# Halving 44 matmuls of the first MLP product in each chunk

## The chip, the cores and the metric

The kernel runs on one core of one Trainium2 chip. The metric is the device time of one execution in microseconds (us); a kernel's time is the median of its runs. One more execution was taken by the hardware profiler, and everything said below about single instructions comes from that one. Engines are named as the profile names them: PE is TensorE's matmul, PEld its weight load, DVE is VectorE, ACT is ScalarE, POOL is GpSimd and SP is SyncE.

## The reference

The program is an RWKV-7 recurrence followed by a two-layer MLP with exact gelu, all in fp32. For each of 4 batches and 8 heads a 40x40 state is carried over 768 steps; the rows of the result, 3072 tokens of 320 values, go through the MLP.

```python
for t in range(S):
    ...
    y[:, :, t] = np.einsum('bhd,bhde->bhe', rt, state)
    Sa = np.einsum('bhde,bhe->bhd', state, at)
    state_decay = state * wt[:, :, None, :] - np.einsum('bhd,bhe->bhde', Sa, bt)
    state = state_decay + np.einsum('bhd,bhe->bhde', vt, kt)
...
h = x @ w_in                                   # 3072x320 by 320x2048
g = 0.5 * h * (1.0 + erf(h * inv_sqrt2))
return (g @ w_out).astype(np.float32)          # 3072x2048 by 2048x320
```

## The kernel before

The 768 steps are cut into 12 chunks (NCH) of 64 (C). Within a chunk the recurrence is written as matrix products for all heads and batches; only the state goes from chunk to chunk. The main loop (line 1244) runs over chunks 2 to 11; chunks 0 and 1 are written out before it, mixed with the conversion of the weights.

**The recurrence's products.** Most go through the helper `mm` (line 110) and are small, 32 or 64 rows by 32 or 64 columns, so that four of them fit on the 128x128 array side by side, each on its own tile of the array. They are named after their PSUM tile: `J` and `J2` (lines 784 to 800), `X` (816), `sap` (828), `saT_ps` (839), `QY` (862 and 874), `M_ps`, `A_ps`, `RV_ps` and `N_ps` (584), `wT_ps` and `cum` (435 and 439), `av` (644). Four products in a row on four different tiles are the rule; `saT_ps` is the exception, since its loop goes over rows e^x in the order 0, 1, 1, 0, so that two products in a row fall on one tile. `tn_ps` (lines 459 and 915) are 8 transposes of 128x128.

**The MLP.** `mlp(c)` (line 985) is a generator. For each quarter q of the 2048 hidden values it makes one PSUM tile `ph` with 20 matmuls (line 993): two blocks s of hidden values, five blocks kt of 64 inputs, two halves x. Half x uses the rows x\*64 to x\*64+63 of the array, of `w_in_sb` and of `xt`, and writes to its own PSUM bank `ph[:, x]`; so two matmuls can run at once, on the upper and the lower half of the array. The moving operand has TB = 256 columns (two groups g of 128 tokens). ACT then takes gelu of the tile into `gt` (line 995). Chunks 0 to 2 finish with a plain second product (line 1010); from chunk 3 (NS) on, `seven` (line 936) makes it with seven block products in place of eight (line 946), 112 matmuls of 160 columns.

**The order of the work.** All queues follow the order of the program text; nothing is moved by a scheduler. `pieces` holds generators of `mlp`, and `fill()` (line 1024) runs the oldest up to its next `yield`, so that a piece of MLP stands between two steps of the recurrence. In a chunk of the main loop PE's order is J, X, a piece of ph, J2, a piece of ph, sap, saT_ps, a piece of ph, the first part of QY, M_ps, a piece of ph, the rest of QY, and then pieces of the second product (`po`) between A_ps, wT_ps, cum, tn_ps, av, RV_ps and N_ps.

**In the machine's program** an fp32 matmul is two passes, each a weight load (LDWEIGHTS) and a matmul (MATMUL) of its own, one after the other. The four instructions of one matmul stand together.

Of the kernel before, what the change touches and what calls it, by code (L numbers as in the profile page):

```python
# [19 lines left out]
def kernel(  # L20
# [46 lines left out]
    nc = tc.nc  # L67
    B, H, S, D = r.shape
    DM, DF = moe_w_in.shape
    P = 128  # L70
# [5 lines left out]
    G = B // 2  # L76
    NCH = S // C
    NF = DF // P
    TB = G * P
    NK = -(-DM // HP)  # L80
# [15 lines left out]
    def duo(name):  # L96
        pt = psum.tile([P, 2, 512], FP32, tag="duo", name=name)
        while asked:
            n = asked.pop()
            mm(pt[:, 0, :n * P], ident, cum_m.unsqueeze(1).to_broadcast([P, n, P]))  # L100
        return pt

    def half(j, n=HP):
        return slice(j * HP, j * HP + n)
# [37 lines left out]
    NS = 3  # L142
# [155 lines left out]
    w_in_sb = const.tile([P, NK, DF // 2], FP32, name="w_in_sb")  # L298
# [620 lines left out]
    def block(g, z):  # L919
        return gt[:, z * NF // 2:(z + 1) * NF // 2, g * P:(g + 1) * P]  # L920
# [12 lines left out]
    def half_tile(tag, bufs):  # L933
        return work.tile([P, NF // 2, P], FP32, tag=tag, name="half", bufs=bufs)
# [47 lines left out]

    gts = {}

    def mlp(c):
        xt = xts.pop(c)
        for q in range(NF // 4):
            ph = duo("ph").rearrange("p x (s t) -> p x s t", s=2)
            for s in range(2):
                p = 2 * q + s  # L990
                for kt in range(NK):
                    for x in range(2):
                        nc.tensor.matmul(ph[:, x, s], w_in_sb[half(x), kt, p * P:(p + 1) * P], xt[half(x), kt],  # L993
                                         start=kt == 0, stop=kt == NK - 1)
            nc.scalar.activation(gt[:, 4 * q:4 * q + 4].rearrange("p (x s) t -> p x s t", x=2), ph, ACT.Gelu)  # L995
            if c >= NS and q == NF // 4 - 1:
                s1, s2 = half_tile("conv", 2), None
                nc.vector.tensor_tensor(s1, block(1, 0), block(1, 1), ALU.add)  # L998
                if c >= NCH - 2:
                    s2 = half_tile("conv", 2)  # L1000
                    nc.vector.tensor_tensor(s2, s1, block(0, 0), ALU.subtract)
            yield
        if c >= NS:
            yield from seven(c, s1, s2)
            return
        po = duo("po")[:, :, :DM]
        for part in range(2):
            for g in range(G):
                for f in range(NF // 2 * part, NF // 2 * (part + 1)):
                    nc.tensor.matmul(po[:, g], gt[:, f, g * P:(g + 1) * P], w_out_sb[:, f],  # L1010
                                     start=f == 0, stop=f == NF - 1)
                for last in range(G if part and g else 0):
                    os = work.tile([P, DM], FP32, tag="os", name="os", bufs=2)
                    nc.vector.tensor_copy(os, po[:, last])
                    for e in range(2):
                        row = (G * e + last) * S + c * C
                        nc.sync.dma_start(out=out[row:row + C], in_=os[half(e)])
                yield
# [118 lines left out]
    fetch(2, "k", k, nc.sync)  # L1137
    fetch_inverse(1)
    pieces.append(mlp(0))
    turn_v(1)  # L1140
    convert(1)
# [23 lines left out]
    turn_b(2)  # L1165
    scale_a(2)
    pieces.append(mlp(1))
    keep(4)
    make_RV(1)
# [74 lines left out]
    for c in range(2, NCH):  # L1244
        n, n2 = c + 1, c + 2
# [52 lines left out]
        make_QY(c)  # L1298
        outputs(c)
        pieces.append(mlp(c))  # L1300
        fill()
        if c == NS:
# [65 lines left out]
```

## Time and profile before

| | us |
|---|---|
| median of 3 runs | 715.56 |
| lowest and highest of them | 711.93, 718.55 |
| the profiled execution | 718.05 |
| its span, first to last instruction | 716.3 |
| PE busy | 670.0 (94%) |
| PEld busy | 586.9 (82%) |
| DVE, ACT, POOL busy | 370.6, 219.8, 354.0 |
| mean granted TensorE clock | 0.962 |

The span is what the traced instructions cover; 1.75 us of the execution lie around it. Busy time is the time in which at least one instruction of the engine was running. A row of a group of instructions has the line, the engine, the operation, the tiles written and read, the shapes and the count, then the busy time in us and the mean of one instruction in ns, then the idle time of the engine just before them and what ended it. "issue" there means that the profile shows nothing that the engine waited for. A row of a table of windows has a stretch in us from the span's start, its length, the busy time and count of PE, PEld, DVE, ACT and POOL, the granted clock, the busy share of the DMA engines and GB/s. A row of the timeline has the start and the length of a run of like instructions, and in brackets the idle time before it. A row of a DMA queue has packets, MB and share of the 16 engines.

### The profile page before, as it was taken

The page shows a single profiled execution, that of the slowest core. Times are in us where ns is not written, and L with a number is a line of the kernel's source. Part 1 is how long each engine was busy: PE and PEld are TensorE (multiplying, and loading weights), DVE is VectorE, ACT ScalarE, POOL GpSimd, SP SyncE. Part 2 cuts the span into 40 slices and gives each one's busy share as a digit, 9 for nine tenths or more (in the row PEclk, how much of TensorE's full clock was granted, in tenths as well). Part 3 has the DMA queues.
Part 4 walks back from the last instruction along what each step waited for, and adds up shares of the span by engine and source line. Part 5 has one row for each costly group of instructions (what it writes and reads, how often), then busy time and mean ns, then how long its engine had stood idle before and what let it go on. Part 6 is the DMA issues. An engine that isn't in the chain of part 4 may idle for free.

```text
span 716.3 us, 32732 instructions
## 1 busy us (share of the span) xinstructions
PE 670.0 (94%) x14778; PEld 586.9 (82%) x14778; DVE 370.6 (52%) x485; ACT 219.8 (31%) x304; POOL 354.0 (49%) x798
## 2 busy tenths in 40 slices
PE   7578897779999999999999999999999999989997
PEld 4477787657777877898899998998898998978987
DVE  2324789974354365374484473672671862521303
ACT  5124664533140240351341332232323403112020
POOL 5384458800851852861853844835826826810000
PEclk9775899989999999999999999999999999999999
DMA  9689447763666657656656647647738635020100
GB/s 129 120 163 157 96 99 189 132 128 80 129 121 107 132 103 104 126 106 110 130 99 120 130 90 132 128 86 132 140 67 151 118 61 107 21 53 4 28 10 19
DMA packets 287923, 74.46 MB, mean 104 GB/s; under 512 B 265736, under 2 KB 284456, under 8 KB 287784
## 3 DMA queue, kind: packets, MB, share of 16 engines
q1 hardware_dynamic: 283360, 68.20, 51.6%
q0 software_dynamic: 864, 2.36, 2.1%
q8 instruction: 116, 1.90, 1.2%
q10 hardware_dynamic: 3560, 1.80, 0.9%
q14 instruction: 23, 0.19, 0.1%
HBM read 58.69 MB, written 9.70 MB: 95 GB/s over the span
## 4 chain that ended last, share of the span: by engine, by line
PE 72%; DVE 5%; POOL 4%; DMA 3%; issue 2%; ACT 1%; ACTq 1%; SPq 0%; DVEq 0%; POOLq 0%
PE ph L993 27%; PE po L946 16%; PE po L1010 7%; PE QY L110 5%; PE J L110 2%; POOL W L674 2%; POOL tmp L672 2%; PE X L110 2%; PE av L110 2%; PE RV_ps L110 1%; PE sap L110 1%; PE saT_ps L110 1%; PE A_ps L110 1%; PE wT_ps L110 1%; PE N_ps L110 1%
## 5 line engine op out<-in xcount | busy, mean ns | idle before, releaser
L993 PE MATMUL ph<-xt,w_in_sb 64*128 64x256 f32 x1920 | 220.5, 381 | 1.3 <-issue 1.3
L672 POOL TENSOR_TENSOR tmp<-W,Nb 128x126 f32<-128x126 f32 (+22 forms) x310 | 126.6, 409 | 161.8 <-DMA Nb<-N 138.8
L993 PEld LDWEIGHTS ph<-xt,w_in_sb 64*128 64x128 f32 x1920 | 183.4, 187 | 23.5 <-issue 2.5
L674 POOL TENSOR_TENSOR W<-W,tmp 128x126 f32<-128x126 f32 (+22 forms) x310 | 133.0, 429 | 24.3
L995 ACT ACTIVATE gt<-ph 128x1024 f32<-128x1024 f32 x48 | 49.1, 1024 | 151.4 <-PE ph L993 151.3
L946 PE MATMUL po<-w_out_sb,gt 128*128 128x160 f32 x576 | 82.9, 302 | 0.1
L946 PEld LDWEIGHTS po<-w_out_sb,gt 128*128 128x128 f32 x576 | 78.7, 190 | 2.2 <-DVE gt L966 0.4
L1010 PE MATMUL po<-w_out_sb,gt 128*128 128x320 f32 x192 | 55.4, 445 | 0.0
L1010 PEld LDWEIGHTS po<-w_out_sb,gt 128*128 128x128 f32 x192 | 36.6, 194 | 15.3 <-issue 1.3
L802 DVE COPY Tt<-J 32x512 f32<-32x512 f32 x11 | 7.6, 689 | 56.4 <-ACT Tt L802 56.3
L186 DVE STREAM_TRANSPOSE aT<-a_pairs 128x1024 f32<-128x1024 f32 x9 | 11.2, 1247 | 44.8 <-DMA a_pairs<-in_a_dram 44.8
L786 ACT COPY Js<-J 128x256 f32<-128x256 f32 x11 | 4.1, 370 | 97.0 <-PE J L110 97.0
L998 DVE TENSOR_TENSOR half<-gt 128x1024 f32<-128x1024 f32 x9 | 11.2, 1242 | 30.0 <-ACT gt L995 30.0
L946 PE MATMUL po<-extra,half 128*128 128x160 f32 x176 | 26.1, 303 | 0.0
L320 ACT ACTIVATE conv<-conv,rebias 128x320 uint32<-128x320 uint32 (+1 forms) x26 | 16.1, 623 | 31.7 <-DVE conv L319 28.7
L995 ACT ACT_TABLE_LOAD x10 | 12.8, 1283 | 38.3 <-PE ph L993 38.2
L946 PEld LDWEIGHTS po<-extra,half 128*128 128x128 f32 x176 | 24.2, 190 | 0.3
L575 DVE TENSOR_TENSOR SM<-M_ps,upper 128x1024 f32<-128x1024 f32 x12 | 14.5, 1208 | 18.4 <-PE M_ps L110 18.4
L950 DVE TENSOR_TENSOR os<-os,po 128x160 f32<-128x160 f32 x36 | 11.4, 317 | 23.4 <-PE po L946 17.7
L662 POOL MEMSET W<- 128x512 f32 x10 | 5.3, 529 | 34.6 <-DMA inv<-W 34.6
L946 PE MATMUL po<-extra,gt 128*128 128x160 f32 x144 | 21.0, 299 | 0.0
L886 DVE TENSOR_TENSOR xt<-QY,wpT 128x512 f32<-128x512 f32 x24 | 15.4, 686 | 9.6 <-PE QY L110 9.2
(223 smaller groups left out, 1134.7 us busy)
## 6 DMA issues: line engine op xcount, KB each, us to landing
Nb<-N SPq DMA_DIRECT2D x20, 256.0 KB
VR<-in_v_dram SPq DMA_DIRECT2D x24, 160.0 KB
out_dram<-os SPq DMA_DIRECT2D x48, 80.0 KB
b_rows<-in_b_dram SPq DMA_DIRECT2D x22, 160.0 KB
k_rows<-in_k_dram SPq DMA_DIRECT2D x22, 160.0 KB
N<-N SPq DMA_DIRECT2D x44, 64.0 KB
Tt<-inv SPq DMA_DIRECT2D x44, 64.0 KB
a_pairs<-in_a_dram SPq DMA_DIRECT2D x18, 144.0 KB
```

What stands on the lines that cost most here:

```text
L110: nc.tensor.matmul(o, lhsT, rhs, start=first, stop=True, skip_group_check=True)
L186: nc.vector.transpose(to.rearrange("p n (s y) -> p n y s", y=2), raws.pop((c, n)).rearrange("p n (y d) -> p n y d", y=2)[:, :, :, :BL])
L320: nc.scalar.activation(power, power, ACT.Relu, bias=rebias, scale=8.0)
L575: nc.vector.tensor_tensor(to, pt, upper.unsqueeze(1).to_broadcast([P, 2 * G * NP, C]), ALU.mult)
L672: eng.tensor_tensor(t, W[:, :rows, j:j + 1].to_broadcast([P, rows, rest]), Nb[:, j:j + 1, j + 1:].to_broadcast([P, rows, rest]), ALU.mult)
L674: eng.tensor_tensor(W[:, :rows, j + 1:], W[:, :rows, j + 1:], t, ALU.add)
L886: nc.vector.tensor_tensor(xt[:, :NP, g * P:(g + 1) * P].rearrange("p i (e t) -> p i e t", e=2), Y, wp[:, g, :, :, :C], ALU.mult)
L946: nc.tensor.matmul(po[:, n, :DM // 2], l_[:, f], r_[:, f], start=f == 0, stop=f == NF // 2 - 1)
L950: nc.vector.tensor_tensor(to, one_, other, ALU.add)
L993: nc.tensor.matmul(ph[:, x, s], w_in_sb[half(x), kt, p * P:(p + 1) * P], xt[half(x), kt], start=kt == 0, stop=kt == NK - 1)
L995: nc.scalar.activation(gt[:, 4 * q:4 * q + 4].rearrange("p (x s) t -> p x s t", x=2), ph, ACT.Gelu)
L1010: nc.tensor.matmul(po[:, g], gt[:, f, g * P:(g + 1) * P], w_out_sb[:, f], start=f == 0, stop=f == NF - 1)
```

## The change

`parts_of(c)` counts the calls for chunk c. Of the matmuls of line 993 with kt = 1, 2 or 3 (48 of 80 in a chunk), the first 44 are issued as two matmuls of 128 columns each, from chunk 4 on; in chunk 3 the first 18; in chunks 0 to 2 none. Both halves use the same weights, loaded again for each. The first and last kt stay whole, since they open and close the accumulation of the PSUM tile. Each chunk from chunk 4 on then has 2560 TensorE instructions, and nothing else is different; line numbers below the edit move by 10.

```diff
@@ -982,6 +982,13 @@
     gts = {}
 
+    parted = {}
+
+    def parts_of(c):
+
+        parted[c] = parted.get(c, 0) + 1
+        return G if parted[c] <= ((0 if c < NS else 18) if c <= NS else 44) else 1
+
     def mlp(c):
...
                 for kt in range(NK):
                     for x in range(2):
-                        nc.tensor.matmul(ph[:, x, s], w_in_sb[half(x), kt, p * P:(p + 1) * P], xt[half(x), kt],
-                                         start=kt == 0, stop=kt == NK - 1)
+                        n = parts_of(c) if 0 < kt < NK - 1 else 1
+                        for g in range(n):
+                            cols = slice(g * TB // n, (g + 1) * TB // n)
+                            nc.tensor.matmul(ph[:, x, s, cols], w_in_sb[half(x), kt, p * P:(p + 1) * P],
+                                             xt[half(x), kt, cols], start=kt == 0, stop=kt == NK - 1)
```

## Prediction

> **What bounds the kernel now.** I read the page first, for the engine that is full.
>
> ```profile
> span 716.3 us, 32732 instructions
> ...
> PE 670.0 (94%) x14778; PEld 586.9 (82%) x14778; DVE 370.6 (52%) x485; ACT 219.8 (31%) x304; POOL 354.0 (49%) x798
> ...
> q8 instruction: 116, 1.90, 1.2%
> ...
> L993 PE MATMUL ph<-xt,w_in_sb 64*128 64x256 f32 x1920 | 220.5, 381 | 1.3 <-issue 1.3
> ```
>
> TensorE is busy 94% of the span. Line 993 is called 960 times but recorded 1920 times: each fp32 matmul is two passes, each with its own weight load. So a chunk's 80 calls are 320 instructions, and 44 more matmuls are 176 more instructions. The queue called instruction moved 116 packets and 1.90 MB: 16 KB, or 256 instructions of 64 bytes, each.
>
> Next I cut the steady part into chunks, from one X product to the next, in the table of windows.
>
> ```profile
> 281.50:331.70 50.20, 50.20 (x1192) 45.59 (x1188) 28.75 (x35) 15.53 (x22) 30.24 (x68) 1.00 0.61 110
> 331.70:383.10 51.40, 50.56 (x1185) 45.73 (x1184) 29.57 (x35) 15.53 (x22) 29.13 (x68) 1.00 0.63 112
> 383.10:433.30 50.20, 50.20 (x1196) 45.59 (x1191) 28.68 (x35) 15.53 (x22) 29.92 (x68) 1.00 0.64 119
> 433.30:484.30 51.00, 50.47 (x1188) 46.12 (x1188) 28.55 (x35) 15.53 (x22) 29.86 (x68) 1.00 0.64 117
> 484.30:535.40 51.10, 50.68 (x1190) 45.82 (x1188) 28.44 (x35) 15.53 (x22) 30.13 (x68) 1.00 0.64 117
> ```
>
> The first two numbers after the window are its length and PE's busy time. An undisturbed chunk is 50.20 us, all PE, at full clock: any nanosecond added to PE there is added to the time. Three chunks are 0.8 to 1.2 us longer. The timeline shows why.
>
> ```profile
> 335.56 0.90 PE L993 MATMUL ph<-xt,w_in_sb 64*128 64x256 f32 x5 [0.84 <-issue]
> ```
> ```profile
> 469.80 0.55 PE L110 MATMUL av<-VR,A 64*64 64x40 f32 x21 [0.54 <-issue]
> ```
> ```profile
> 488.59 1.24 PE L993 MATMUL ph<-xt,w_in_sb 64*128 64x256 f32 x9 [0.42 <-issue]
> ```
>
> "issue" means that PE waited for nothing that the profile shows. Counted along TensorE's records these stalls stand at instructions 13,762, 20,161 and 20,929: 6,399 and 768 apart, 25 and 3 blocks of 256 (one off, as records are in order of time). In each, an instruction packet had landed 1.4 to 1.5 us before. So PE ran out of instructions at a block's edge. From start to start the stalls took 1.22, 0.76 and 0.79 us, where 0.22, 0.03 and 0.22 are usual: 2.3 us lost.
>
> **What the Trainium skill says.** "Runtime: NRT & Kernel Launch", Instruction fetch mechanics: an engine's instructions stream in blocks of 16 KiB, 256 instructions, and crossing an edge is mostly hidden. The trace agrees on the size, and on mostly: three stalls after 240 us.
> "TensorE: Matmul & The Clock Gate", Part 3: weight loads overlap running matmuls only on another row group, and matmuls are strictly first in, first out. The trace differs on both. At 402.52 the first two line-993 matmuls start 7 ns apart, then the next two together 0.3 us later, although the program's order is pass 1 and pass 2 of x=0, then both of x=1: x=1's first pass overtook x=0's second. And a load for a row half starts 1 to 2 ns after that half's matmul.
> "TensorEngine Tiling (Array Packing)", Key Properties: tiles load and multiply independently. The trace agrees: each half starts a 256-column pass every 216 ns, both at once.
>
> **The change part by part.**
>
> *Passes.* 18 + 8 x 44 = 370 matmuls are halved, in 185 pairs (x=0, x=1). A pair was four 256-column passes, two at a time: 2 x 216 = 432 ns. It becomes eight 128-column passes, each with a load of the same 128 columns: four slots if the halves still run together. The nearest row for a slot is the transposes on line 459, 128 columns with a 128-column load each: starts 109.2 ns apart. 4 x 109.2 = 437 ns, +4.8 ns a pair, +0.9 us in all. This is PE time, so it all counts.
>
> *Order.* The loop over g is innermost, so four passes go to one row half, then four to the other. To keep both halves busy PE must overtake further than now. saT_ps (line 839) already has this: its order gives runs of four passes on one 64x64 tile, loads as long as matmuls. sap before it never has more than two.
>
> ```profile
> 393.89 1.14 PE L110 MATMUL sap<-avs,Tt 64*64 64x40 f32 x64
> 394.85 1.20 PE L110 MATMUL saT_ps<-Tt,avs 64*64 64x64 f32 x64
> ```
>
> Both have 64 passes in nearly the same time, which four tiles at once need. The steady spacing of M_ps (line 848, runs of two, 64 columns as well) is 14.1 ns a pass, of saT_ps 15.1: runs of four cost 7%. Upper end: 437 x 1.07 - 432 = 36 ns a pair, +6.7 us. Lower end 0.9: the columns streamed are the same, so halving can't gain. I take 8 ns, +1.5 us, since two tiles need less overtaking than four.
>
> *Fetch.* A chunk had 2384 TensorE instructions in the trace, 9.3 blocks, so edges wandered; now ten edges stand at the same places in every chunk. Counting the changed program from the edge that stalled: within J2, sap, ph, M_ps, QY, A_ps, tn_ps, RV_ps, po, X. PE holds some 64 instructions ahead, so a block is asked for when PE is 64 before an edge and needed 256 after it. After 240 us the packet started 2.1 us (median) after that first point, took 1.1, and served 1.4 after landing: 4.6 us, 3.7 to 6.0 for nine in ten. The stretches that the new edges give are 4.7 us (sap to ph), 5.5 (ph to M_ps; A_ps to tn_ps), 5.7 and 5.8, all others over 6.4. Near the tightest place five fetches needed 3.4 to 4.8. I expect 0.15 us of stalls a chunk, 1.2 us over eight, against 2.3: -1.1 us. Ends: -2.3 (none left) to +1.7 (0.5 us a chunk).
>
> *Hidden parts.* 1480 more instructions are six packets, 95 KB of 74.46 MB. They are added where PE spends over 50 ns an instruction, so they don't crowd the queue. No wait, DMA or step of another engine is added or moved; ACT's gelu (line 995) waits for ph 151 us in all, so ACT isn't late. Chunks 0 to 2 are untouched.
>
> Sum: +1.5 - 1.1 = +0.4 us on the profiled execution's 718.05 us: 718.4. That execution lay 2.5 us over the median of its three runs (715.56), so the median after is **716.0 us**.
>
> **The rivals.**
> *Overlap lost (slower).* If PE can't reach x=1's passes while x=0's later ones are queued, each half starts only when the other's last pass starts: six slots, 655 ns for 432, +223 ns a pair, +41 us: 757 us. It decides at a reach of two pending instructions per tile. For it: the skill's first in, first out, and that ph itself has only runs of two. Against: saT_ps; strict order would give it runs nearly twice as long as M_ps.
> *Dear halves and a bad edge (slower, smaller).* The upper ends of passes and fetch together: 6.7 + 1.7 = +8.4: 724 us. The edges are the same in each chunk, so one bad edge costs eight times.
> *Edges all quiet.* No stall left, halves at 109.2: -2.3 + 0.9 = -1.4: 714 us. For it: no stretch lies clearly below the usual 4.6. It lies within 1%.
> That the change doesn't do what it says is excluded by the program: 2384 + 176 = 2560.
>
> **How the numbers follow.** A measurement of this kernel can tell about 1% (7.2 us) from no change; its three runs spread over 6.6. Forecast 0.60, quiet edges 0.17, overlap lost 0.13, dear halves 0.07, a gain over 1% that nothing here explains 0.03. Faster 0.03, same 0.77, slower 0.20. The range goes from 711 (quiet edges, 714, less half the spread of the runs) to 724 (dear halves) and leaves out lost overlap and the unexplained gain.
>
> **What would show it.** Right: undisturbed chunks of 50.2 to 50.6 us; halved passes 109 to 113 ns apart on each row half, two running; issue gaps of PE after 300 us 0 to 3 us in sum, at the same place of each chunk. Wrong: a chunk of 55 us, with three of its four pieces of ph at 5.9 instead of 4.5 us (lost overlap), or a gap before ph, M_ps or tn_ps in each chunk (bad edge).

## The result

The changed kernel's median is 721.52 us (15 runs, 718.33 to 723.84), that of the kernel before 716.31 in 15 runs beside it (711.93 to 720.33). The ratio is 1.0067, with a 95% interval of 1.0048 to 1.0086: slower by 4.8 us, 3.4 to 6.2. Ratios are estimated without runs that lie over 1.5% above the fastest of their kernel (four of the 22 of e6 below, none elsewhere), so they can differ from the quotient of two medians. The forecast was no difference that can be told (+0.4 us). The sign is now plain, the size lies under 1%, and most of it is one term that I took too small.

The page of the changed kernel, its head and two groups of the matmuls:

```profile
span 719.8 us, 34212 instructions
...
PE 674.9 (94%) x15518; PEld 603.0 (84%) x15518; DVE 367.4 (51%) x485; ACT 219.6 (31%) x304; POOL 345.3 (48%) x798
...
q8 instruction: 122, 2.00, 1.2%
...
L1003 PE MATMUL ph<-xt,w_in_sb 64*128 64x128 f32 (+1 forms) x2660 | 226.1, 323 | 0.1
...
L946 PE MATMUL po<-w_out_sb,gt 128*128 128x160 f32 x576 | 82.9, 302 | 1.1 <-DVE gt L966 1.1
```

There are 740 more matmul records and six more instruction packets, as counted beforehand. PE is busy 4.9 us longer. The idle time ahead of ph has gone from 1.3 to 0.1 us, and a wait that was not there has come: po for gt.

The table of windows, chunks 4 to 8 of the changed kernel, then chunk 9, then all from the last X product to the end (the "tail", with the MLP of the last two chunks). A window is named after the chunk whose MLP it holds; its recurrence is one chunk ahead.

```profile
333.30:384.80 51.50, 51.12 (x1284) 47.67 (x1272) 28.45 (x35) 15.53 (x22) 28.82 (x68) 1.00 0.64 116
384.80:435.80 51.00, 51.00 (x1282) 47.66 (x1272) 28.52 (x35) 15.53 (x22) 28.98 (x68) 1.00 0.64 118
435.80:486.70 50.90, 50.90 (x1284) 47.54 (x1273) 28.38 (x35) 15.52 (x22) 28.62 (x68) 1.00 0.63 117
486.70:537.70 51.00, 51.00 (x1282) 47.57 (x1272) 28.56 (x35) 15.54 (x22) 28.96 (x68) 1.00 0.64 117
537.70:588.60 50.90, 50.90 (x1284) 47.54 (x1273) 28.13 (x35) 15.54 (x22) 29.12 (x68) 1.00 0.63 115
588.60:637.60 49.00, 48.58 (x1144) 45.56 (x1136) 19.50 (x26) 9.76 (x14) 30.02 (x65) 1.00 0.37 62
637.60:719.80 82.20, 76.77 (x1242) 73.51 (x1232) 19.12 (x31) 11.65 (x18) 0.00 (x0) 0.99 0.07 18
```

The last two rows in the kernel before:

```profile
585.80:636.30 50.50, 47.85 (x1056) 43.56 (x1050) 21.76 (x29) 9.77 (x14) 29.76 (x65) 1.00 0.35 62
636.30:716.30 80.00, 75.57 (x1062) 69.57 (x1056) 19.10 (x31) 11.65 (x18) 0.00 (x0) 1.00 0.07 18
```

The chunks have become even: four of five take 50.9 to 51.0 us, all PE. But that even chunk is 0.75 us longer than the undisturbed one of before (50.87 against 50.12, from start of X to start of X). The tail is 2.2 us longer.

Where the 3.5 us between the two profiled spans lie, by starts of X: up to chunk 3 +1.0, chunk 3 +0.7, chunks 4 to 8 +1.1, chunk 9 -1.5, tail +2.2. Two of these aren't the change's. The code before chunk 3 is the same in both, and its length differs from execution to execution (276 to 285 us over all profiles here). In chunk 9 the kernel before waited 2.3 us for DVE (J for L of line 772); another profile of unsplit matmuls (e5 below) has no such wait and takes 48.1 us there.

Chunks 4 to 8 hold two things. The first is seen in one piece of ph, of before and then of after, in the timeline:

```profile
384.18 4.59 PE L993 MATMUL ph<-xt,w_in_sb 64*128 64x256 f32 x40
```
```profile
385.89 4.78 PE L1003 MATMUL ph<-xt,w_in_sb 64*128 64x256 f32 x64
```

40 records have become 64, and the piece is 0.19 us longer, with no gap in it. Three pieces of a chunk have 12 split matmuls, the fourth has 8 and is 0.16 us longer: 0.73 us a chunk, or 33 ns for each of 22 pairs. Chunks 4 to 10 have that seven times; chunk 3 adds 0.34 us and the last chunk 0.43: 5.9 us over the 185 pairs.

The second is the stalls at block edges. What chunks 4 to 8 took beyond five undisturbed ones was 3.5 us before and is 0.9 after; one issue gap is left in them:

```profile
353.44 0.58 PE L110 MATMUL M_ps<-rT,saT 40*64 40x64 f32 x24 [0.38 <-issue]
```

In the tail, passes explain 1.2 us: four pieces by 0.73, and the last chunk's ph in one run, 17.90 us instead of 17.47. The rest is a chain that ends at po. The timeline of all engines, after and then before:

```profile
669.69 3.57 ACTq L897 DMA_DIRECT2D xt<-xt  x4
...
673.36 0.29 ACT L961 COPY os<-po 128x160 f32<-128x160 f32 x1 [9.88 <-issue]
...
674.12 1.22 DVE L966 TENSOR_TENSOR gt<-gt,half 128x1024 f32<-128x1024 f32 x1
...
675.39 1.90 PE L946 MATMUL po<-w_out_sb,gt 128*128 128x160 f32 x12 [1.12 <-DVE gt L966]
```
```profile
667.63 2.56 ACTq L897 DMA_DIRECT2D xt<-xt  x4
...
670.29 0.29 ACT L961 COPY os<-po 128x160 f32<-128x160 f32 x1 [8.87 <-DMA xt<-xt]
...
671.06 1.22 DVE L966 TENSOR_TENSOR gt<-gt,half 128x1024 f32<-128x1024 f32 x1
...
672.33 1.90 PE L946 MATMUL po<-w_out_sb,gt 128*128 128x160 f32 x12
```

ACT issues four transfers for the last chunk before it copies po. They took 3.57 us instead of 2.56, so ACT's copies, DVE's sum behind them and PE's next product all came 1 us later. One issue of the four makes the difference, here after and then before:

```profile
671.01 1.60 ACTq L897 DMA_DIRECT2D xt<-xt  x1
```
```profile
668.95 0.60 ACTq L897 DMA_DIRECT2D xt<-xt  x1
```

### The profile page after: what moved, and what is told of

Same layout as the page of the kernel before. It is cut to its first block, busy times and chain, and to the rows that moved or that the text cites. A ratio compares the mean times of both kernels' runs of the same rounds, so it can differ in the third digit from the quotient of the medians.

```text
span 719.8 us, 34212 instructions
## 1 busy us (share of the span) xinstructions
PE 674.9 (94%) x15518; PEld 603.0 (84%) x15518; DVE 367.4 (51%) x485; ACT 219.6 (31%) x304; POOL 345.3 (48%) x798
## 4 chain that ended last, share of the span: by engine, by line
PE 79%; DVE 4%; DMA 1%; ACT 1%; issue 1%; ACTq 1%; SPq 0%; DVEq 0%
PE ph L1003 30%; PE po L946 18%; PE po L1020 7%; PE QY L110 6%; PE J L110 2%; PE X L110 2%; PE av L110 2%; PE RV_ps L110 2%; PE sap L110 1%; PE saT_ps L110 1%; PE A_ps L110 1%; PE M_ps L110 1%; PE N_ps L110 1%; PE wT_ps L110 1%; PE tn_ps L459 1%
## 5 line engine op out<-in xcount | busy, mean ns | idle before, releaser
L1003 PE MATMUL ph<-xt,w_in_sb 64*128 64x128 f32 (+1 forms) x2660 | 226.1, 323 | 0.1
L1003 PEld LDWEIGHTS ph<-xt,w_in_sb 64*128 64x128 f32 x2660 | 199.5, 187 | 11.8 <-issue 1.3
L672 POOL TENSOR_TENSOR tmp<-W,Nb 128x126 f32<-128x126 f32 (+22 forms) x310 | 122.1, 394 | 169.7 <-DMA Nb<-N 146.7
L674 POOL TENSOR_TENSOR W<-W,tmp 128x126 f32<-128x126 f32 (+22 forms) x310 | 129.8, 419 | 24.3
L830 DVE COPY SM<-sap 128x640 f32<-128x640 f32 x12 | 9.9, 824 | 23.2 <-PE sap L110 23.2
```

Of the source, the lines that this page charges most:

```text
L672: eng.tensor_tensor(t, W[:, :rows, j:j + 1].to_broadcast([P, rows, rest]), Nb[:, j:j + 1, j + 1:].to_broadcast([P, rows, rest]), ALU.mult)
L674: eng.tensor_tensor(W[:, :rows, j + 1:], W[:, :rows, j + 1:], t, ALU.add)
L1003: nc.tensor.matmul(ph[:, x, s, cols], w_in_sb[half(x), kt, p * P:(p + 1) * P], xt[half(x), kt, cols], start=kt == 0, stop=kt == NK - 1)
```

## The experiments

The runs are called e1 to e12, and the two kernels before and after. Each ratio is to runs of the kernel before on the same chip. Spans and stretches are of one profiled execution. "Excess" is what chunks 4 to 8 took beyond five undisturbed chunks of that same kernel (of the changed kernel, where it has none undisturbed); it holds every wait, not only those at block edges. The kernel before was some 2 us faster beside the first four runs (714.34) than beside the changed kernel (716.31), which lowers medians against those expected; the ratios are free of this.

**Is it the order of the halves?** The loops over g and x are exchanged: the same calls, but the two row halves of the array take turns at every call.

```diff
                 for kt in range(NK):
-                    for x in range(2):
-                        n = parts_of(c) if 0 < kt < NK - 1 else 1
-                        for g in range(n):
+                    n = [parts_of(c) if 0 < kt < NK - 1 else 1 for x in range(2)][1]
+                    for g in range(n):
+                        for x in range(2):
```

> The two loops are swapped: for each half g the two matmuls of x=0 and x=1 follow one another, so that the four calls of a pair go 0, 1, 0, 1 over the row halves and not 0, 0, 1, 1. Instructions and block edges are as in the changed kernel. My theory (halves are dear because of the runs of four passes on one row half, and the edges at fixed places are quiet): a split piece of ph falls from 4.71 to at most 4.56 us, a chunk from 50.87 to 50.2 to 50.4, and the median to 714 to 716.5, at or below the kernel before. Rival 'no slack' (a 128-column pass with a 128-column load of its own takes 111.7 ns in any order): pieces stay at 4.60 to 4.71, chunk at least 50.6, median 718 to 721.5. Rival 'edges' (the loss comes from instruction fetch): pieces fall or not, the median stays at 721.

e1: median 718.08 against 714.34, ratio 1.0052 (1.0033 to 1.0072). A piece of ph and the longest waits of PE:

```profile
496.94 4.68 PE L1003 MATMUL ph<-xt,w_in_sb 64*128 64x256 f32 x64
```
```profile
PE QY L110 <- DVE SM L575: 4.6, 2, 3.2
```

A piece takes 4.61 us from its start to that of the next product, between 4.52 and 4.71. So the 33 ns of a pair have two halves. With runs of four passes on a row half, one row half begins and ends a slot later than the other, 0.10 us a piece; turns take that away. The other 0.09 us stays: 24 slots of a piece are 111.7 ns each, where half of a 256-column pass is 108. The undisturbed chunk is 50.45 us, 0.42 less than in the changed kernel, as it should be. Yet the kernel wasn't that much quicker: this execution lost 4.6 us because QY waited for DVE's mask SM, and DVE stood in front of a transpose whose input had not landed.

```profile
509.03 1.25 DVE L186 STREAM_TRANSPOSE aT<-a_pairs 128x1024 f32<-128x1024 f32 x1 [12.08 <-DMA a_pairs<-in_a_dram]
510.20 1.18 DVE L575 TENSOR_TENSOR SM<-M_ps,upper 128x1024 f32<-128x1024 f32 x1
```

**Where the halves end.** Three more kernels change how many matmuls are split, and so where the block edges stand: 48 in each chunk from chunk 4 on (2576 instructions, so that edges wander), 22 (2472), and 44 with 38 more in chunk 2, which brings every later edge 152 instructions earlier in the work.

```diff
-        return G if parted[c] <= ((0 if c < NS else 18) if c <= NS else 44) else 1
+        return G if parted[c] <= ((0 if c < NS else 18) if c <= NS else 48) else 1
```

> All 48 matmuls with kt 1 to 3 are split from chunk 4 on, not 44, so a chunk has 2576 TensorE instructions and the block edges move by 16 from chunk to chunk. My theory (cost is per split pair, and fixed edges save about 1.7 us of stalls): all four pieces at 4.71, undisturbed chunk 50.9, and issue gaps return in some chunks, 1 to 5 us in sum; median 722 to 726. Rival 'no gain from fixed edges': only the two further pairs a chunk count, +0.3 us: 721.5 to 722.

e2: median 718.10 against 714.34, ratio 1.0054 (1.0033 to 1.0075); four pieces of 4.71 us a chunk, excess 0.8 us. The expected 722 to 726 was too high. With edges that wander by 64 instructions over chunks 4 to 8 it does no worse than with edges that stand still, so these runs don't show that standing still is what quiets them.

```diff
-        return G if parted[c] <= ((0 if c < NS else 18) if c <= NS else 44) else 1
+        return G if parted[c] <= ((38 if c == NS - 1 else 0) if c < NS else 18 if c == NS else 44) else 1
```

> As the changed kernel, with 38 matmuls of chunk 2 split as well: 152 more TensorE instructions before the steady part, so that the fixed edges stand 152 instructions earlier in every chunk, at a place where the trace of the changed kernel gives three short stretches per chunk (3.75, 3.84 and 4.53 us, where a fetch needs 3.7 to 6.0). My theory (PE stalls where a block is used up before the next is there): issue gaps at the same places in each of chunks 4 to 9, 0.8 to 2 us a chunk; chunk 51.7 to 52.9 us, median 728 to 737. Rival 'edges are nearly always hidden' : only the 38 split matmuls count, +0.6 us: 722.

e3: median 726.66 against 714.34, ratio 1.019 (1.0157 to 1.0223). Part of a piece of ph in the timeline, and the waits of PE between 240 and 670 us:

```profile
391.83 2.79 PE L1003 MATMUL ph<-xt,w_in_sb 64*128 64x256 f32 x34 [0.86 <-issue]
```
```profile
PE ph L1003 <- issue: 5.8, 6, 1.7
PE av L110 <- issue: 1.2, 3, 0.6
```

The first ph piece of chunks 4 to 9 took 5.5 to 6.9 us instead of 4.71, and the excess is 9.8 us. By the count of instructions, three stretches between edges are 3.8, 3.8 and 4.5 us long here, below the 4.6 us that a block needs from demand to use. Less 0.6 us for the 19 pairs in chunk 2, these are the changed kernel's passes, moved against the edges, and they cost a further 1.1%: the fetch is real, and its place is what counts. The median lies below the expected 728, the chunks (52.2 to 54.0 us) at and above what was expected.

```diff
-        return G if parted[c] <= ((0 if c < NS else 18) if c <= NS else 44) else 1
+        return G if parted[c] <= ((0 if c < NS else 18) if c <= NS else 22) else 1
```

> Only 22 matmuls are split from chunk 4 on, not 44: 2472 TensorE instructions a chunk, edges move by 88 back from chunk to chunk. My theory: two pieces of ph dear (4.71 and about 4.69), two at 4.52, so an undisturbed chunk is 50.17 + 0.35 = 50.5; half of the passes' loss (3 us in place of 6) and the kernel before's stalls of about 2 us: median 718.5 to 721. Rival 'edges' (the loss comes from the fixed edges): about the kernel before, 716 to 717.

e4: median 720.26 against 714.34, ratio 1.0082 (1.0058 to 1.0105). Pieces of 4.71, 4.70, 4.52 and 4.52 us: half the cost in passes. But two pieces took 6.8 and 6.7 us, and the excess is 4.3 us. The waits of PE:

```profile
PE ph L1003 <- issue: 3.0, 2, 1.5
```

What half of the splitting saves is lost again in these two pieces.

**Take the late transpose away.** The transpose of a and the transfer behind it move from before M's mask to after it in DVE's and SP's order; in the kernel before, in the alternating one, and in the changed one.

```diff
-        if more2:
-            turn_a(n2)
-            fetch_pairs(n2, "b_turned", b, nc.sync, False, paired["a"])
         fill()
         make_y2(c)
         make_M(c)
+        if more2:
+            turn_a(n2)
+            fetch_pairs(n2, "b_turned", b, nc.sync, False, paired["a"])
```

> The kernel before, with the transpose of the state input a (and the fetch that reuses its buffer) put behind the mask of M in VectorE's queue, so that a late transfer of a no longer holds the mask, and with it QY, back. Control for the next two. My theory (the wait for a decides only where PE runs ahead of the transfers): 0.996 to 1.001 of the kernel before. Rival (the move itself delays b's transfer and with it the transposes of the next chunk): over 1.002.

The kernel before with this step moved (e5): median 712.86 against 712.49, ratio 1.0008 (0.9989 to 1.0028). No difference. The undisturbed chunk stays at 50.12 us, the tail at 80.0, and the wait of J in chunk 9 is absent.

> The alternating order of the first experiment, with the same move of the transpose of a behind the mask of M. Theory 'late a' (the alternating kernel's shorter pieces are given back in waits of QY for the mask, 4.6 us in its trace): no wait of QY for the mask, ratio to the kernel before 0.999 to 1.003. Rival 'chance' (those waits were this one execution's): as without the move, 1.004 to 1.007.

The alternating order with it (e6): median 718.28 of all 22 runs against 712.49, ratio 1.0065 (1.0041 to 1.0089). QY no longer waits for the mask, and nothing is gained: a late a isn't why the alternating order falls short. What the profile has in its place is the edge at M_ps:

```profile
PE M_ps L110 <- issue: 1.4, 3, 0.5
```

> The changed kernel with the same move. Its trace has no wait of QY for the mask, so by my theory the move gains little: 1.004 to 1.007 of the kernel before, pieces of ph at 4.71. Rival (runs other than the profiled one wait for a): 1.001 to 1.003.

The changed kernel with it (e8): median 718.56 against 712.49, ratio 1.0079 (1.005 to 1.0109). Two of its chunks:

```profile
333.60:384.50 50.90, 50.90 (x1291) 47.57 (x1284) 28.33 (x35) 15.57 (x23) 29.22 (x68) 1.00 0.63 118
384.50:435.30 50.80, 50.80 (x1282) 47.47 (x1276) 28.21 (x35) 15.34 (x23) 28.82 (x68) 1.00 0.63 116
```

Chunks 4 to 8 of this execution have next to no stall (excess 0.06 us): four take 50.87 us and one 50.93, and the kernel is still slower than before. With these edges quiet, the passes are what costs there, 0.75 us a chunk.

**Has the load any slack?** In the alternating order, a matmul is cut into 192 and 64 columns in place of 128 and 128. The columns and the loads are as many as before.

```diff
-                            cols = slice(g * TB // n, (g + 1) * TB // n)
+                            cols = slice(0, TB) if n == 1 else slice(g * 192, 192 + g * 64)
```

> The alternating order, but the split matmuls are cut into 192 and 64 columns, not 128 and 128. Theory 'load has no slack' (a slot lasts as long as the longer of a pass and a weight load of 128 columns): slots of 162 and about 110 ns, a pair 2 x (162 + 110) = 544 in place of 447 ns, split pieces of ph at 5.1 to 5.3 us, chunk 52.3 to 52.9. Rival 'a price per instruction' (each pass costs its columns and 3 to 5 ns): pieces as with 128 and 128, 4.58 to 4.65.

One execution (e7): 738.97, with 712.49 for the kernel before. One piece:

```profile
443.08 5.29 PE L1003 MATMUL ph<-xt,w_in_sb 64*128 64x256 f32 x64
```

Start to start a piece is 5.22 us, 0.70 over the whole matmuls' 4.52. If a pass of 64 columns lasts as long as its load of 128 columns, 110 ns, and one of 192 columns 162 (three quarters of 216), a pair takes 2 x 272 = 544 ns instead of 432, and six pairs add 0.67 us. Had the load any room, 64 columns would have taken 54 ns. The loads show it directly: on one row half they start 110 to 112 ns apart around the 64-column passes and 162 to 164 around the 192-column ones. So the 111.7 ns of a 128-column slot is the pace of the load, a little over the 108 of the pass.

**Alternating order, other edges.** 20 split matmuls in chunk 3 in place of 18, which moves the edge out of M_ps; and 48 in each chunk.

```diff
-        return G if parted[c] <= ((0 if c < NS else 18) if c <= NS else 44) else 1
+        return G if parted[c] <= ((0 if c < NS else 20) if c <= NS else 44) else 1
```

> The alternating order with 20 split matmuls in chunk 3, not 18: the fixed edges move by 8 instructions, so that the stretch up to the edge in M_ps, at which the alternating kernel with the moved transpose had three gaps of about 0.5 us, grows from 5.42 to 5.58 us (the one from sap to ph shrinks from 4.91 to 4.75). Theory 'fast pieces use up a block sooner' (the alternating order's gain is eaten by waits at the edge in M_ps): fewer gaps, chunks mostly at 50.45, ratio to the kernel before 1.001 to 1.004. Rival 'something else than edges': 1.004 to 1.007 as before, with gaps or without.

e9: median 718.92 against 713.59, ratio 1.0082 (1.005 to 1.0114). The profiled execution was as expected: chunks of 50.4 to 50.8 us, no issue gap of PE after 240 us, 714.03 us. It was also the shortest of its six; the others took 715.8 to 721.5.

```diff
-        return G if parted[c] <= ((0 if c < NS else 18) if c <= NS else 44) else 1
+        return G if parted[c] <= ((0 if c < NS else 18) if c <= NS else 48) else 1
```

> The alternating order with all 48 matmuls split from chunk 4 on: 2576 TensorE instructions a chunk, edges that wander by 16 a chunk. To be compared with the 48 in the order of the changed kernel (1.0054). Theory 'cost per pass and skew': four pieces at 4.61 in place of 4.71, 0.4 us a chunk less, 3.4 us in all: 1.000 to 1.002. Rival 'the gain of the alternating order is given back' (to fetch or to late transfers): 1.003 to 1.006.

e10: median 718.82 against 713.59, ratio 1.007 (1.0038 to 1.0103). Pieces of 4.61 us; the last chunks gave part of it back, with gaps in ph and 1.4 us of QY waiting for the mask. Both runs are slower than expected, and both kernels as slow as the changed one.

**The microsecond in the tail.** The long stretch of issues on ACT's queue (3.4 to 3.6 us for four) and PE's wait of 0.9 to 1.2 us are in the five profiles with 44 halved matmuls in each chunk at the changed kernel's edges or 8 instructions from them (after, e1, e6, e8, e9), in e7 with 3.8 and 1.4 us, and not in before, e2, e3, e4, e5 and e10. Two kernels try it: one splits 36 matmuls in the eleventh chunk, which moves the tail's edges by 32 instructions; one has SP issue those transfers.

```diff
-        return G if parted[c] <= ((0 if c < NS else 18) if c <= NS else 44) else 1
+        return G if parted[c] <= ((0 if c < NS else 18) if c <= NS else 36 if c == NCH - 2 else 44) else 1
```

> In the changed kernel's tail ACT's third transfer issue of line 897 took 1.60 us instead of 0.60, ACT's copies at line 961 came 1.0 us later for it, and PE's po waited 1.1 us for gt of line 966. Here the eleventh chunk splits 36 matmuls instead of 44, so that in the tail TensorE's block edges stand 32 instructions earlier in the work. Theory that this long issue goes with where the edges of TensorE's instruction blocks fall: the issue takes 0.6 us again, PE does not wait for gt, and the stretch from the last X to the end is 82.2 - 1.1 - 0.13 (four pairs at 33 ns) = 81.0 us. Rival, that it goes with the splitting itself (the later pace of the last chunk): the long issue and the 1.1 us wait stay, 82.1 us. The total, of one execution, tells nothing: 716 to 724.

```profile
672.35 2.57 ACTq L897 DMA_DIRECT2D xt<-xt  x4
```

In e11 the issues take 2.57 us again and PE doesn't wait. The tail is 83.8 us all the same, since this execution met a stretch of lower clock at its beginning:

```profile
637.60:646.30 8.70, 8.70 (x146) 8.02 (x141) 1.25 (x3) 0.37 (x1) 0.00 (x0) 0.65 0.16 40
```

X took 1.94 us there instead of 1.14, and the first ph 6.74 instead of 4.78. Without these 2.8 us the tail is 81.1 us, as expected. So the long issue goes with the edges and not with the splitting; e3, with the same 44 matmuls at other edges, had none either.

The traces also show what an edge brings with it. In each of the six profiles with a long issue, a 16 KB instruction packet for TensorE starts 0.03 to 0.22 us after that issue has begun (at 671.04 in the changed kernel), and the issue ends 0.3 to 0.4 us after the packet has landed. In before, e2, e3, e4, e5, e10 and e11 no such packet overlaps ACT's issues of lines 894 and 897. SP's issues agree: those of over 1 us that overlap such a packet, 1212 in the 14 profiles, end 0.40 us (median) after it has landed. By what path the packet holds the issue isn't shown. The Trainium skill ("Perfetto Trace Analysis", DMA Instruction — HWDGE) counts into an issue's length the wait for a descriptor generator that queues share; but in the changed kernel SP's last issue had ended at 670.66, before the long one began at 671.01.

```diff
-            eng = nc.scalar if x and c == NCH - 1 else nc.sync
+            eng = nc.sync
```

> The last chunk's transfers of line 894 and 897 that ACT issues are issued by SP instead, behind SP's own. Theory that PE's wait for gt comes from ACT's queue alone: ACT copies at line 961 as soon as its operands are there, PE does not wait for gt, and the stretch from the last X to the end is 82.2 - 1.1 = 81.1 us; xt is needed 9 us after the last issue would end, so SP's longer queue costs nothing. Rival, that the wait moves (DVE is late for another reason, or SP's queue is late for xt and the last ph waits): 82.2 us or more. The total, of one execution, tells nothing: 716 to 724.

```profile
670.43 0.29 ACT L961 COPY os<-po 128x160 f32<-128x160 f32 x1 [6.47 <-PE po L946]
...
671.19 1.22 DVE L966 TENSOR_TENSOR gt<-gt,half 128x1024 f32<-128x1024 f32 x1
...
674.57 4.51 PE L946 MATMUL po<-w_out_sb,gt 128*128 128x160 f32 x32
```

In e12 ACT copies as soon as po is there, PE follows without a gap, and the tail is 80.8 us instead of 82.2. The wait did come from ACT's queue. As one execution each, these two took 723.19 and 720.60 us; no kernel of this study was faster than the kernel before.

## Why the prediction was right or wrong

The terms of its sum, and what they measured:

| term | forecast, us | measured, us |
|---|---|---|
| passes, 185 pairs | +1.5 (8 ns each) | +5.9 (32 ns each) |
| stalls at block edges | -1.1 | -1.9 |
| ACT's queue in the tail | 0 | +1.1 |
| sum | +0.4 | +5.1 |
| timed | | +4.8 (3.4 to 6.2) |

The stalls are the mean excess of chunks 4 to 8, all waits included: 3.5 and 1.6 for the unsplit kernel (before, e5), 0.9, 0.06, 0.5 and 1.4 for the split one (after, e8, e11 and e12, which have the same passes there).

**Passes: the step that failed** is "I take 8 ns, +1.5 us, since two tiles need less overtaking than four". It measured 32 ns, +5.9 us. The bounds were 4.8 and 36 ns, and I went to the lower one with an argument that no row supported. The runs give the cost two parts. About half of it is the order: one row half starts a slot late, 0.10 us once in every piece however many matmuls are split, and e1 removes just that. The other half is the load, which takes 110 to 112 ns (e7), so that a slot takes 111.7; I had 109.2 from the transposes, and 108 is what halving would have to reach to be free.

That the upper bound came so near is luck. It put the order at 7% of every pass, and its row was misread: the 14.1 ns for M_ps is not the steady spacing. In steady state M_ps starts a pass every 14.6 ns, and so does saT_ps from its 33rd pass on; saT_ps is 0.09 us longer from its first start to its last (0.98 us against 0.90). Runs of four cost it something once in a product, not in every pass, as in ph; whether it is the same slot isn't shown.

**Order.** That the halves would overlap was right. Passes on the two row halves start 1 to 2 ns apart even with runs of four on a half, again unlike the strict first in, first out of the Trainium skill ("TensorE: Matmul & The Clock Gate", Part 3). The rival of lost overlap, 757 us, falls: its pieces would have been 5.9 us, and they are 4.71.

**Fetch.** The direction was right in these profiles, and the size was cautious. That the edges became quiet because they stand still is not shown: e2's wander and have an excess of 0.8 us. The 64 instructions from which a demand is counted were not measured either; the packets of before follow any point 36 to 68 instructions ahead of an edge about equally steadily (within 0.8 to 0.9 us). The tightest stretch, sap to ph, didn't stall in chunks 4 to 9; e3 shows that shorter ones do. "Dear halves and a bad edge" was thus half true, dear halves alone. "Edges all quiet" came nearly true for the edges, and gave no 714 us because it had cheap halves in it.

**Hidden parts.** "No wait, DMA or step of another engine is added or moved" failed in the tail: ACT's queue, PE's wait for gt, 1.1 us. The six added packets were counted there as bytes; where one of them falls was not. That ACT had 151 us of idle time said nothing of one place where it issues transfers just before a copy that PE needs.

**The range** held the time, since it took in dear halves. That the change stayed within 1% was forecast rightly, but with a sum 4.4 us too low, and partly by luck: the passes alone, at four times their forecast, take most of that 1%, and the quieter edges gave 2 us back.

**What stays open.** The alternating order saves 0.4 us a chunk in every profile, some 3 us, and its four kernels (1.0052, 1.0065, 1.0082, 1.0070) are no better than the order of the change (1.0067, 1.0079, 1.0054). Part of it is seen: its excess was 5.6, 2.1, 0.35 and 2.0 us, a mean of 2.5, against 0.7 for the order of the change (after, e2, e8, e11, e12), so in the profiles 1.8 us went back into stalls and waits. That shorter pieces leave the fetch and DVE less time is a guess from this. What is left, about 1 us, is no more than the intervals allow, and the timed executions, which no profile shows, vary by 7 us.

## What to carry to other kernels

Splitting a matmul pays a weight load for each part; where the load takes longer than the shorter pass, the load sets the pace, and with the order of the halves that came to 32 ns a pair here. A place in which PE is full has no small terms: find the nearest row with the same order of tiles, see whether its price comes with every pass or once in a product, and don't discount it without a row that says so. Stalls at instruction blocks were smaller with the edges of the change, but what moves the edges has to cost less than the stalls did (2 us of 716 here), and edges put in the wrong place cost more than all of them. An instruction packet can also delay a transfer issue on another engine's queue, and so a copy behind it.

## What the runs showed of the hardware

- A shift of all block edges by 152 instructions cost 1.1% (1.019 against 1.0067, less the 0.6 us of passes added with it). With stretches of 3.8, 3.8 and 4.5 us of work between edges, one piece of ph in each of chunks 4 to 9 was 0.8 to 2.2 us longer.
- A pass of fp32 with a 128-column load has a floor of 110 to 112 ns: a pass of 64 columns (e7) took as long as one of 128 (e1).
- Runs of four passes on one row half don't end the overlap; they shift one half by a slot, 0.10 us at each change of product.
- One transfer issue on ACT's queue took 1.4 to 1.9 us instead of 0.6 in the six profiles in which an instruction packet for TensorE was under way during it, and in none of the seven others.
- The granted clock goes to half in slices of 3.4 us, as the Trainium skill has it ("TensorE: Matmul & The Clock Gate", Part 1: half rate after an idle window of some 3.4 us). The profiled executions had 14 to 20 such slices in the first 200 us, with nearly the same code there, which may be part of why chunk 3 started between 276 and 285 us. e11 met two more at 637 us, just after PE had waited 2.0 us, less than such a window, and they cost 2.8 us; the kernel before waited 2.3 us at the same place and met none.
